# One partial sum of exponentials per half and head, a weight conversion that goes through PSUM banks, and nine buffers for exponentials

## The chip, the core and the metric

The kernel runs on one core of one Trainium2 chip. The metric is the time of one execution on the device in microseconds. TensorE (PE in the profile; PEld is its loading of weights), VectorE (DVE), ScalarE (ACT), GpSimd (POOL) and SyncE (SP, which issues most DMAs) each work through a list of instructions of their own, in order, and wait for each other with semaphores.

## What is computed

Attention in which a query sees only keys of its own hash bucket, over 4 batches of 8 heads with 768 positions of 64 numbers, and then a two-layer network with a rational activation:

```python
mask = q_bucket[:, :, :, None] == k_bucket[:, :, None, :]
scores = np.where(mask, scale * np.matmul(q, k.transpose(0, 1, 3, 2)), -1000000000.0)
scores = scores - np.max(scores, axis=-1, keepdims=True)
attn = np.exp(scores)
attn = attn / (np.sum(attn, axis=-1, keepdims=True) + 1e-09)
x = heads_side_by_side(np.matmul(attn, v))
...
h = x @ w_in
g = (a0 + a1*h + a2*h*h + a3*h*h*h) / (1 + abs(b0)*abs(h) + abs(b1)*h*h + 1e-6)
return g @ w_out
```

The weights `w_in` and `w_out` come in 64 bits per number. The kernel turns them into a 32-bit number and splits that into a high and a low part for TensorE; this is the work that the text calls the conversion.

## The kernel before

**Pairs, halves, steps.** The 32 heads are worked on as 16 pairs `p`. The scores of a pair are made transposed, with keys on partitions: 2 halves of 384 queries by 6 tiles of 128 keys give 12 steps `s` (steps 0 to 5 are half 0, steps 6 to 11 half 1). A step makes the scores of both heads (`pss`, two matmuls for each head, L356 to L381), ScalarE writes their exponentials into a buffer `E`, and GpSimd adds the exponentials up. After each six steps `values` (L383) multiplies the six buffers by V in 24 matmul passes (`psv`), and `values_out` (L392) has ScalarE read the result (`col`, then `xo`).

**Sums.** Six key tiles of a half are added in two groups of three (`PARTS = 2`): for each group and head one add `acc<-E,E` and one `acc<-acc,E`. So a pair has 4 tiles `acc`, each for both heads, out of a ring of `ACCS = 5`. `sums` (L402), two and a half steps into the next pair, multiplies every `acc` of the pair by a matrix of ones on TensorE (`psu`), the two groups accumulating in PSUM, and ScalarE copies the result out (`sr`). Step 11 of pair 14 and all of pair 15 have the second head's adds on VectorE (L380).

**Work two pairs ahead.** In the same steps TensorE and VectorE find the row maxima of pair p+2: `psm` (two matmuls into one of two double banks), then VectorE's `TENSOR_REDUCE m<-psm`. After step 5 the 12 maxima of pair p+1 are transposed (`pst`) and VectorE turns them into rows (`mt`). VectorE also makes the low parts `lo` of q and k.

**The conversion** (`weights`, L433) runs over 32 pieces, about two in each pair: even ones of `w_in`, odd ones of `w_out`. A piece needs two ScalarE activations (`ws<-wr`, `wr<-wr`), VectorE's `TENSOR_SCALAR wr<-wr` (the sign bits), `SCALAR_TENSOR_TENSOR ws<-ws,wr` (shift and or), an integer add `ws<-wr,ws` on 16-bit limbs (in the profile `CUSTOM_DVE_ANT_0`, in the order `ISA`), then ScalarE's cast to the high part and VectorE's subtraction for the low part (`wi_lo<-ws,wi_hi` or `wr<-ws,wr`). All operands are in SBUF.

**PSUM.** One pool, `ps_b`, has three banks with tag `s` that the scores `pss`, the transposes `pst` and the sums `psu` take in turn, and one bank for `psv`.

**The order** is written out: each piece of work is put at a place `12*p + step` by the tables `FIRST`, `MID` and `LAST`, and the program is issued sorted by that number (L475 to L543). So a wait in one engine's list holds up all that stands behind it there.

After the attention, from 393.6 us on, the two-layer network runs. Its code and order are not touched. The helper that records instructions makes every row of the profile carry line 95.

Of the kernel before, what the change touches and what calls it, by code (L numbers as in the profile page):

```python
# [7 lines left out]
F32 = mybir.dt.float32  # L8
F32R = mybir.dt.float32r
BF16 = mybir.dt.bfloat16  # L10
I32 = mybir.dt.int32
# [23 lines left out]
BIG = 2.0 ** 60  # L35
CLAMP = 2.0 ** 40
PINNED = ("tensor", "vector", "scalar", "gpsimd", "sync")
PARTS = 2
ACCS = 5

MID = dict(
    group=6, values=[0.66, 0.05], values_out=[0.69, 0.06],
    maxima=[6.54, 7.17, 8.32, 9.1, 10.1, 11.02, 12.25, 13.03, 14.15, 15.17, 16.01, 17.43], sums=14.65, sums_store=17.37,
    high=[-0.975, 1.19], low=[1.06, 2.8, 3.35], bits=2.81, penalties=4.02, high_move=1.9, maskrows=4.03, second_low=-2.2,
    second_high=2.69, load_v=10.99, shift_turn=5.67, shift_rows=8.82, load=4.04, recips=[20.0, 35.02, 35.3],
    weights=[[1.44, 5.1, 5.5, 5.65, 5.68, 11.02, 11.035], [8.05, 11.03, 11.04, 11.5, 12.38, 14.29, 17.645, 19.32, 21.22]],
    weights_last=[0.5, 0.8, 1.0, 1.2],
)

# [125 lines left out]
def attention(ctx, tc, nc, raw, ps_b, tail, tokens, early, operands_to_terms, ffn, load, QF, KF, v, w_in, w_out, wo_d, ident, cst, ones, prj,  # L175
# [9 lines left out]
    sm = ctx.enter_context(tc.tile_pool(name="sm", bufs=1))  # L185
    ps_a = ctx.enter_context(tc.tile_pool(name="ps_a", bufs=2, space=PSUM))

    E = [ep.tile([P, 2, HQ + 2], F32, name=f"E{i}") for i in range(7)]
    for e in E:
        nc.gpsimd.memset(e[:, :, HQ : HQ + 2], TINY)  # L190

# [228 lines left out]
    def recips(bb):  # L420
# [9 lines left out]
        nc.sync.dma_start(r_d[bb].rearrange("h (x c) -> (h x) c", c=n), s)  # L430
        yield

    def weights(i):  # L433

        if i % 2 == 0:
            f, cc = divmod(i // 2, 4)
            sl = slice(f * 512, f * 512 + 512)
            src, hi, lo = w_in[cc * P : cc * P + P, sl], wi_hi[:, cc, sl], wi_lo[:, cc, sl]  # L440
        else:
            src, hi, lo = w_out[i // 2 * P : i // 2 * P + P, :], None, None
        r = sm.tile([P, 2 * 512], F32, tag="wr", name=f"wr{i}", bufs=2)
        t = sm.tile([P, 512], F32, tag="ws", name=f"ws{i}", bufs=2)
        if src.dtype == F32:
            nc.sync.dma_start(t, src)
            yield
        else:
            nc.sync.dma_start(r.bitcast(I32), src.bitcast(I32))
            yield  # L450
            hw, lw = r[:, 1:1024:2], r[:, 0:1024:2]
            nc.scalar.activation(t, hw, AF.Copy, scale=2.0 ** -112)
            yield
            nc.scalar.activation(lw.bitcast(I32), lw.bitcast(U32), AF.Copy, scale=2.0 ** -29)
            nc.vector.tensor_scalar(out=hw.bitcast(I32), in0=hw.bitcast(I32), scalar1=-(1 << 31), scalar2=None,
                                    op0=ALU.bitwise_and)
            yield
            nc.vector.scalar_tensor_tensor(out=t.bitcast(I32), in0=t.bitcast(I32), scalar=3, in1=hw.bitcast(I32),
                                           op0=ALU.logical_shift_left, op1=ALU.bitwise_or)
            yield  # L460
            nc.vector.tensor_tensor(out=t.bitcast(I32), in0=t.bitcast(I32), in1=lw.bitcast(I32), op=ALU.add)
            yield
        if hi is None:
            hi, lo = r[:, 0:512].bitcast(F32R), r[:, 512:1024].bitcast(F32R)
        nc.scalar.copy(hi, t)
        yield
        nc.vector.tensor_tensor(out=lo, in0=t, in1=hi.bitcast(F32), op=ALU.subtract)
        yield
        if i % 2 == 1:
            move(nc, wo_d[i // 2], r.rearrange("p (t c) -> p t c", t=2))  # L470
            yield
# [51 lines left out]
    for i in range(2 * NFC):  # L523
        o = 12 * (i // 2)
        w = list(FIRST["weights"][i]) if i < 2 else list(MID["weights"][i % 2])
        if i == 2:
            w = list(FIRST["third_weights"])
        if i == 2 * NFC - 4:
            w[0] = LAST["weights14"]
        if i == 2 * NFC - 3:  # L530
            w[5] = LAST["hi14"]
        if i == 2 * NFC - 2:
            w[1:3] = LAST["weights15"]
        if i == 2 * NFC - 1:
            w = w[:-4] + [w[-5] + x for x in MID["weights_last"]]
        spread(0, [o + x for x in w], weights(i))

    for c in range(3):
# [309 lines left out]
```

## Time and profile before

| | us |
|---|---|
| median of 3 runs (923.38 to 923.84) | 923.7 |
| span of the profiled execution | 921.5 |
| attention, to the first matmul of the network | 393.6 |
| network | 527.9 |
| PE busy | 915.5 |
| DVE busy | 841.5 |
| ACT busy | 653.8 |
| POOL busy | 426.3 |

The page gives the busy time of each engine, then the span in 40 slices with the busy share of each in tenths, then the chain of work that ended last, then groups of equal instructions. In a group, `out<-in` are the program's tiles, `x` counts instructions, and behind the bar stand busy time in us, the mean of one in ns, and the idle time of the engine just before them with what ended it. The sums' matmuls count twice there (128 in the program, x256 in the profile). The profiled span and the time of the profiled execution differ: 923.7 is the median time on the device, the span runs from the first to the last instruction.

### The profile page before, as it was taken

What the parts mean: (1) busy time and instruction counts of PE and PEld (TensorE: products, weight loads), DVE (VectorE), ACT (ScalarE), POOL (GpSimd) and SP (SyncE); (2) the same over time, 40 slices, a digit from 0 to 9 for tenths busy, and PEclk for the clock granted to TensorE, in tenths of its full rate; (3) what the DMA queues carried; (4) which work ended last, traced back from release to release, by engine and by line L of the source; (5) the groups of instructions that cost most, each with busy time, mean ns of one, the idle gap of its engine ahead of it and who ended that gap; (6) DMA issues with size and microseconds to landing.
All of it is one profiled execution on the core that took longest, in us unless ns stands there. A gap on an engine that the chain in (4) does not pass through costs nothing.

```text
span 921.5 us, 13665 instructions
## 1 busy us (share of the span) xinstructions
PE 915.5 (99%) x4671; PEld 699.2 (76%) x4671; DVE 841.5 (91%) x1022; ACT 653.8 (71%) x1227; POOL 426.3 (46%) x363
## 2 busy tenths in 40 slices
PE   9999999999999999999999999999999999999998
PEld 5567767676767676678888888888888888888886
DVE  6799989999899899788998999999999989998997
ACT  7467777777777776976767677767676777667664
POOL 7577777677777777712222222222222222322221
PEclk9999999999999999999999999999999999999999
DMA  7877878787878778555403000400040013001001
GB/s 205 210 214 224 234 205 240 219 236 214 240 209 235 199 213 242 158 191 163 138 1 108 31 1 1 137 1 0 1 137 1 1 43 95 1 1 46 1 0 47
DMA packets 51242, 111.57 MB, mean 121 GB/s; under 512 B 9346, under 2 KB 20214, under 8 KB 51172
## 3 DMA queue, kind: packets, MB, share of 16 engines
q1 hardware_dynamic: 50740, 110.47, 40.7%
q8 instruction: 37, 0.61, 0.3%
q14 instruction: 33, 0.27, 0.1%
q10 hardware_dynamic: 432, 0.23, 0.1%
HBM read 56.82 MB, written 21.17 MB: 85 GB/s over the span
## 4 chain that ended last, share of the span: by engine, by line
PE 99%; DVE 1%; issue 0%; ACT 0%; DVEq 0%
PE psh L95 28%; PE pso L95 28%; PE pss L95 15%; PE psv L95 14%; PE psm L95 8%; PE psu L95 2%; PE psb L95 1%; PE psw L95 1%; PE pst L95 0%; PE pst_None L95 0%; PE psb_first L95 0%; DVE m L95 0%; DVE ws L95 0%; DVE k L95 0%; DVE mb L95 0%
## 5 line engine op out<-in xcount | busy, mean ns | idle before, releaser
L95 POOL TENSOR_TENSOR gl<-c,gh 128x512 fp32r<-128x512 f32 x95 | 135.8, 1429 | 384.9 <-ACT gh L95 374.8
L95 PE MATMUL pso<-wo,gh 128*128 128x512 f32 x768 | 235.9, 389 | 0.0
L95 DVE TENSOR_REDUCE m<-psm 128x1 f32<-128x768 f32 x192 | 181.3, 953 | 28.7 <-PE psm L95 20.1
L95 ACT ACTIVATE E<-pss 128x384 f32<-128x384 f32 x384 | 167.1, 492 | 41.5 <-PE pss L95 33.5
L95 POOL TENSOR_TENSOR acc<-E,E 128x384 f32<-128x384 f32 x124 | 147.2, 1206 | 92.1 <-ACT E L95 92.1
L95 PE MATMUL pss<-q,k 128*128 128x384 f32 (+2 forms) x768 | 171.0, 346 | 0.2
L95 PEld LDWEIGHTS pso<-wo,gh 128*128 128x128 f32 x768 | 144.1, 188 | 29.9
L95 ACT ACTIVATE h<-psh 128x512 f32<-128x512 f32 x96 | 57.4, 598 | 133.1 <-PE psh L95 133.0
L95 PEld LDWEIGHTS pss<-q,k 128*128 128x128 f32 (+2 forms) x768 | 134.5, 190 | 21.3 <-issue 8.0
L95 PE MATMUL psh<-xh,wi_hi 128*128 128x512 f32 x384 | 149.6, 390 | 0.0
L95 PE MATMUL psh<-xl,wi_hi 128*128 128x512 f32 x384 | 149.4, 389 | 0.0
L95 PE MATMUL psh<-xh,wi_lo 128*128 128x512 f32 x384 | 149.4, 389 | 0.0
L95 PE MATMUL pso<-wo,gl 128*128 128x512 f32 x384 | 148.9, 389 | 0.0
L95 DVE SCALAR_TENSOR_TENSOR c<-c,ab,r 128x512 f32<-128x512 f32 x96 | 138.7, 1444 | 0.0
L95 POOL TENSOR_TENSOR acc<-acc,E 128x384 f32<-128x384 f32 x123 | 132.0, 1093 | 3.8 <-ACT E L95 3.4
L95 PE MATMUL psv<-E,v 128*64 128x385 f32 x768 | 131.9, 492 | 0.0
L95 PE MATMUL psm<-k,q 76*128 76x384 f32 (+1 forms) x384 | 101.0, 345 | 0.5 <-ACT q L95 0.2
L95 PEld LDWEIGHTS psv<-E,v 128*64 128x64 f32 x768 | 52.0, 137 | 65.1 <-issue 62.4
L95 DVE SCALAR_TENSOR_TENSOR w<-h,absb,w 128x512 f32<-128x512 f32 x96 | 72.8, 758 | 15.5 <-ACT w L95 15.2
L95 PEld LDWEIGHTS psh<-xh,wi_hi 128*128 128x128 f32 x384 | 72.0, 188 | 16.1 <-issue 1.2
L95 PEld LDWEIGHTS psh<-xl,wi_hi 128*128 128x128 f32 x384 | 72.1, 188 | 15.0
L95 PEld LDWEIGHTS pso<-wo,gl 128*128 128x128 f32 x384 | 72.1, 188 | 15.0
(77 smaller groups left out, 1212.9 us busy)
## 6 DMA issues: line engine op xcount, KB each, us to landing
q<-q SPq DMA_DIRECT2D x45, 192.0 KB
k<-k SPq DMA_DIRECT2D x45, 192.0 KB
wr<-w_in SPq DMA_DIRECT2D x16, 512.0 KB
wr<-w_out SPq DMA_DIRECT2D x16, 512.0 KB
wo_d<-wr SPq DMA_DIRECT2D x16, 512.0 KB
wo<-wo_d SPq DMA_DIRECT2D x16, 512.0 KB
qkf<-qT SPq DMA_DIRECT2D x16, 384.0 KB
qkf<-kT SPq DMA_DIRECT2D x16, 384.0 KB
```

The source lines that it names most:

```text
L95: return self.tc.keep_in_program_order(issue(*args, **kwargs))
```

## The change

With `PARTS = 1` all six tiles of a half go into one `acc` for each head; the ring has 3 tiles. There are nine buffers `E`. For pieces 3 to 27 of the conversion the sign bits go to a bank `psx` with tag `s`, shift-and-or reads and writes that bank, and the limb add reads it; a new ScalarE copy puts the high part into another such bank, `psz`, and VectorE's subtraction reads that. One number of the table moves the limb add of odd pieces ahead of the next maximum; the last piece keeps its old place.

```diff
-PARTS = 2
-ACCS = 5
+PARTS = 1
+ACCS = 3
+BANKED = (3, 28)
...
-    weights=[[...], [8.05, 11.03, 11.04, 11.5, 12.38, 14.29, 17.645, 19.32, 21.22]],
+    weights=[[...], [8.05, 11.03, 11.04, 11.5, 11.6, 14.29, 17.645, 19.32, 21.22]],
...
-    E = [ep.tile([P, 2, HQ + 2], F32, name=f"E{i}") for i in range(7)]
+    E = [ep.tile([P, 2, HQ + 2], F32, name=f"E{i}") for i in range(9)]
...
+    def bank(name):
+        return ps_b.tile([P, 512], F32, tag="s", bufs=3, name=name)
...
-            nc.vector.tensor_scalar(out=hw.bitcast(I32), in0=hw.bitcast(I32), scalar1=-(1 << 31), scalar2=None,
-                                    op0=ALU.bitwise_and)
+            x = y = bank(f"psx{i}").bitcast(I32) if BANKED[0] <= i < BANKED[1] else hw.bitcast(I32)
+            if not BANKED[0] <= i < BANKED[1]:
+                y = t.bitcast(I32)
+            nc.vector.tensor_scalar(out=x, in0=hw.bitcast(I32), scalar1=-(1 << 31), scalar2=None, op0=ALU.bitwise_and)
             yield
-            nc.vector.scalar_tensor_tensor(out=t.bitcast(I32), in0=t.bitcast(I32), scalar=3, in1=hw.bitcast(I32),
-                                           op0=ALU.logical_shift_left, op1=ALU.bitwise_or)
+            nc.vector.scalar_tensor_tensor(out=y, in0=t.bitcast(I32), scalar=3, in1=x, op0=ALU.logical_shift_left,
+                                           op1=ALU.bitwise_or)
             yield
-            nc.vector.tensor_tensor(out=t.bitcast(I32), in0=t.bitcast(I32), in1=lw.bitcast(I32), op=ALU.add)
+            nc.vector.tensor_tensor(out=t.bitcast(I32), in0=y, in1=lw.bitcast(I32), op=ALU.add)
...
-        nc.vector.tensor_tensor(out=lo, in0=t, in1=hi.bitcast(F32), op=ALU.subtract)
+        z = hi.bitcast(F32)
+        if BANKED[0] <= i < BANKED[1]:
+            z = bank(f"psz{i}")
+            nc.scalar.copy(z, hi.bitcast(F32))
+        nc.vector.tensor_tensor(out=lo, in0=t, in1=z, op=ALU.subtract)
...
-            w = w[:-4] + [w[-5] + x for x in MID["weights_last"]]
+            w = w[:-5] + [12.38 + x for x in [0.0] + MID["weights_last"]]
```

In the rows below the numbers in `pss8_6_1` are pair, step and head, in `psx16` the piece; numbers after the last underscore only tell tiles apart. In brackets stand the semaphores that a row waits for: `DVE_49` is VectorE's, `Activation_49` ScalarE's, `Pool_49` GpSimd's, the ones with DMA are transfers.

**Place A**, TensorE in pair 8 behind the values of half 0 (the transpose of the maxima, then steps 6 and 7). Before:

```order
L95 MATMUL pst9_None_2715<-cst_75,m9_2451 12x128 [waits DVE_49]
L95 MATMUL pss8_6_0_2724<-q1_8_1990,k1_8_2045 128x384
L95 MATMUL pss8_6_0_2724<-q2_8_2234,k2_8_2235 128x384
L95 MATMUL pss8_6_1_2728<-q1_8_1990,k1_8_2045 128x384
L95 MATMUL pss8_6_1_2728<-q2_8_2234,k2_8_2235 128x384
L95 MATMUL psm10_0_2733<-k1_10_2595,q1_10_2541 128x384 [waits DMAHW4_49,DMAHW5_49,DMAHW3_49,PE_49]
L95 MATMUL psm10_0_2733<-k1_10_2595,q1_10_2541 128x384
L95 MATMUL pss8_7_0_2737<-q1_8_1990,k1_8_2045 128x384 [waits DVE_49]
L95 MATMUL pss8_7_0_2737<-q2_8_2234,k2_8_2235 128x384
L95 MATMUL pss8_7_1_2741<-q1_8_1990,k1_8_2045 128x384 [waits Activation_49]
```

Now:

```order
L96 MATMUL pst9_None_2744<-cst_75,m9_2476 12x128 [waits DVE_49]
L96 MATMUL pss8_6_0_2753<-q1_8_2008,k1_8_2066 128x384 [waits DVE_49]
L96 MATMUL pss8_6_0_2753<-q2_8_2257,k2_8_2258 128x384
L96 MATMUL pss8_6_1_2757<-q1_8_2008,k1_8_2066 128x384 [waits DVE_49]
L96 MATMUL pss8_6_1_2757<-q2_8_2257,k2_8_2258 128x384
L96 MATMUL psm10_0_2762<-k1_10_2624,q1_10_2567 128x384 [waits DMAHW4_49,DMAHW5_49,DMAHW3_49,PE_49]
L96 MATMUL psm10_0_2762<-k1_10_2624,q1_10_2567 128x384
L96 MATMUL pss8_7_0_2766<-q1_8_2008,k1_8_2066 128x384 [waits Activation_49]
L96 MATMUL pss8_7_0_2766<-q2_8_2257,k2_8_2258 128x384
L96 MATMUL pss8_7_1_2770<-q1_8_2008,k1_8_2066 128x384 [waits DVE_49]
```

The banks differ. Before, steps 6 take two free banks and head 0 of step 7 the bank of `pst9`, once `mt9` has read it. Now step 6 head 0 takes the bank of `psz15` (waits for the subtraction), head 1 the bank of `pst9` (waits for `mt9`), step 7 head 0 the bank of step 6 head 0 (waits for its exponential) and head 1 that of `psx16` (waits for the limb add). The same pattern stands in pairs 2 to 13.

**Place B**, TensorE at the start of pair 9, behind the values of half 1 of pair 8. Before:

```order
L95 MATMUL pss9_0_0_2848<-q1_9_2272,k1_9_2326 128x384 [waits DMAHW6_49]
L95 MATMUL pss9_0_0_2848<-q2_9_2503,k2_9_2504 128x384 [waits DMAHW1_49]
L95 MATMUL pss9_0_1_2852<-q1_9_2272,k1_9_2326 128x384
L95 MATMUL pss9_0_1_2852<-q2_9_2503,k2_9_2504 128x384 [waits DMAHW7_49,DMAHW0_49]
L95 MATMUL psm10_6_2856<-k1_10_2595,q1_10_2541 128x384 [waits DMAHW5_49,DVE_49]
L95 MATMUL psm10_6_2856<-k1_10_2595,q1_10_2541 128x384
L95 MATMUL pss9_1_0_2861<-q1_9_2272,k1_9_2326 128x384
L95 MATMUL pss9_1_0_2861<-q2_9_2503,k2_9_2504 128x384
L95 MATMUL pss9_1_1_2865<-q1_9_2272,k1_9_2326 128x384 [waits Activation_49]
```

Now:

```order
L96 MATMUL pss9_0_0_2882<-q1_9_2294,k1_9_2351 128x384 [waits DMAHW6_49]
L96 MATMUL pss9_0_0_2882<-q2_9_2530,k2_9_2531 128x384 [waits DMAHW1_49]
L96 MATMUL pss9_0_1_2886<-q1_9_2294,k1_9_2351 128x384 [waits DVE_49]
L96 MATMUL pss9_0_1_2886<-q2_9_2530,k2_9_2531 128x384 [waits DMAHW7_49,DMAHW0_49]
L96 MATMUL psm10_6_2890<-k1_10_2624,q1_10_2567 128x384 [waits DMAHW5_49,PE_49]
L96 MATMUL psm10_6_2890<-k1_10_2624,q1_10_2567 128x384
L96 MATMUL pss9_1_0_2894<-q1_9_2294,k1_9_2351 128x384 [waits Activation_49]
L96 MATMUL pss9_1_0_2894<-q2_9_2530,k2_9_2531 128x384
L96 MATMUL pss9_1_1_2898<-q1_9_2294,k1_9_2351 128x384 [waits Activation_49]
```

Step 0 head 1 now takes the bank of `psz16` (waits for the subtraction). Step 1 head 0, which had a free bank, now takes that of step 0 head 0 and waits for its exponential; `psx17` holds the third bank. So it stands at the start of pairs 3 to 13; at the start of pairs 2 and 14 a row of step 1 waits for the limb add instead.

**VectorE at place B**, from the subtraction of piece 16 on. Before:

```order
L95 TENSOR_TENSOR wi_lo_127<-ws16_2598,wi_hi_126 128x512
L95 TENSOR_SCALAR wr17_2765<-wr17_2765 128x512
L95 SCALAR_TENSOR_TENSOR ws17_2766<-ws17_2766,wr17_2765 128x512
L95 TENSOR_REDUCE m10_2732<-psm10_6_2856 128x1
L95 ISA ws17_2766<-wr17_2765,ws17_2766 128x1024
```

Now:

```order
L96 TENSOR_TENSOR wi_lo_127<-ws16_2627,psz16_2857 128x512
L96 TENSOR_SCALAR psx17_2861<-wr17_2794 128x512
L96 SCALAR_TENSOR_TENSOR psx17_2861<-ws17_2795,psx17_2861 128x512
L96 ISA ws17_2795<-wr17_2794,psx17_2861 128x1024
L96 TENSOR_REDUCE m10_2761<-psm10_6_2890 128x1
```

Each of the four conversion rows now has one operand in a bank, and the limb add has moved ahead of the maximum of step 6.

More of the change, by code (lines that the diff above doesn't have):

```diff
@@ L45 @@
     second_high=2.69, load_v=10.99, shift_turn=5.67, shift_rows=8.82, load=4.04, recips=[20.0, 35.02, 35.3],
-    weights=[[1.44, 5.1, 5.5, 5.65, 5.68, 11.02, 11.035], [8.05, 11.03, 11.04, 11.5, 12.38, 14.29, 17.645, 19.32, 21.22]],
+    weights=[[1.44, 5.1, 5.5, 5.65, 5.68, 11.02, 11.035], [8.05, 11.03, 11.04, 11.5, 11.6, 14.29, 17.645, 19.32, 21.22]],
     weights_last=[0.5, 0.8, 1.0, 1.2],
```

## The prediction

> **What bounds the kernel now.** I read the page first: the share of each engine, then the chain that ended last.
>
> ```profile
> PE 915.5 (99%) x4671; PEld 699.2 (76%) x4671; DVE 841.5 (91%) x1022; ACT 653.8 (71%) x1227; POOL 426.3 (46%) x363
> ...
> PE 99%; DVE 1%; issue 0%; ACT 0%; DVEq 0%
> PE psh L95 28%; PE pso L95 28%; PE pss L95 15%; PE psv L95 14%; PE psm L95 8%; PE psu L95 2%; PE psb L95 1%; PE psw L95 1%; PE pst L95 0%; PE pst_None L95 0%; PE psb_first L95 0%; DVE m L95 0%; DVE ws L95 0%; DVE k L95 0%; DVE mb L95 0%
> ```
>
> TensorE is never idle to speak of, and `psu`, which the change halves, stands on the chain with 2%. The windows view over twelve pairs of the attention shows who could take over (columns: length, then busy us and instructions of each engine, granted clock, DMA):
>
> ```profile
> core 0: us, PE busy (x) PEld busy (x) DVE busy (x) ACT busy (x) POOL busy (x), PEclk, DMA share, GB/s
> 75.60:357.20 281.60, 281.60 (x1741) 198.31 (x1740) 253.76 (x292) 206.46 (x450) 213.41 (x193) 1.00 0.79 223
> ```
>
> A pair takes 281.6 / 12 = 23.47 us of TensorE without a gap, 21.1 of VectorE, 17.2 of ScalarE, 17.8 of GpSimd. So a matmul that goes saves its whole time, and a wait that TensorE gets costs its whole time. That is the account to draw up. 0.2% of the median is 1.85 us, about what a measurement of this kernel can tell from no change.
>
> **Saved: half of the sums' matmuls.** The timeline of TensorE at one sum and the row behind it:
>
> ```profile
> 216.48 1.50 PE L95 MATMUL psu<-acc,ones 128*32 128x384 f32 x16
> 217.79 1.47 PE L95 MATMUL psb<-qkf,prj 128*32 128x384 f32 x16
> ```
>
> Sixteen passes hold TensorE for 217.79 - 216.48 = 1.31 us. With one `acc` instead of two it is eight, 0.65 less. There are 16 sums: 16 x 0.65 = **10.4 us saved**, since nothing on TensorE waits there.
>
> **What one wait costs.** Of the new waits in the order rows above, the trace of before has both kinds, a score matmul that waits for an exponential and one that waits for `mt`:
>
> ```profile
> 359.86 0.86 PE L95 MATMUL pss<-q,k 77*128 77x384 f32 x4
> 360.88 0.50 ACT L95 ACTIVATE E<-pss 128x384 f32<-128x384 f32 x1
> 360.91 1.14 PE L95 MATMUL pss<-q,k 77*128 77x384 f32 x4
> 361.43 0.30 PEld L95 LDWEIGHTS pss<-q,k 77*128 77x128 f32 x2 [0.32 <-ACT E L95]
> 66.44 0.27 DVE L95 TENSOR_SCALAR mt_None<-pst_None 12x128 fp32r<-12x128 f32 x1
> 66.76 0.65 PEld L95 LDWEIGHTS pss<-q,k 77*128 77x128 f32 x4 [0.45 <-DVE mt_None L95]
> ```
>
> The exponential ends at 361.38, TensorE goes on at 361.43; `mt` ends at 66.71, TensorE goes on at 66.76: 0.05 from end to start. Four score matmuls with such a wait take 1.14 where an undisturbed four take 0.86. Of these 0.28 the wait itself is 0.18 (from the 361.25 at which the third of four, 0.175 apart, was due), and 0.10 is lost in restarting, since no weights were loaded ahead.
>
> **Place A, waits for `mt`.** The rows of pair 8, where the banks change hands:
>
> ```profile
> 226.61 0.28 PE L95 MATMUL pst_None<-cst,m 128*12 128x128 f32 x1
> 226.64 0.96 PE L95 MATMUL pss<-q,k 77*128 77x384 f32 x4
> 226.92 0.28 DVE L95 TENSOR_SCALAR mt_None<-pst_None 12x128 fp32r<-12x128 f32 x1 [0.28 <-PE pst_None L95]
> 227.08 0.34 PE L95 MATMUL pss<-q,k 77*128 77x384 f32 x1
> 227.13 0.67 DVE L95 CUSTOM_DVE_ANT_0 ws<-wr,ws 128x1024 uint16<-128x1024 uint16 x1
> 227.42 0.48 ACT L95 ACTIVATE E<-pss 128x384 f32<-128x384 f32 x1
> ```
>
> Head 1 of step 6 starts at 227.08 and will need `mt`, which ends at 227.20: it goes on at 227.25, 0.18 late, and with the restart 0.28. What is queued behind it, a maximum and step 7, moves by as much. Step 7 head 0, due 0.7 after 227.08, needs the exponential that ends at 227.90 and comes at 228.06: no wait. Head 1, 0.35 behind it at 228.41, needs the limb add, done at 227.80. The subtraction that head 0 of step 6 needs stands ahead of `mt` on VectorE, which was idle for 0.28 before `mt`: done. Twelve pairs: 12 x 0.28 = **3.4 us lost**.
>
> **Place B, waits for an exponential.** The start of pair 9:
>
> ```profile
> 237.15 0.97 PE L95 MATMUL pss<-q,k 77*128 77x384 f32 x4
> 237.29 0.16 ACT L95 COPY col<-psv 128x1 f32<-128x1 f32 x1 [1.06 <-PE psv L95]
> 237.97 0.48 ACT L95 ACTIVATE E<-pss 128x384 f32<-128x384 f32 x1
> 238.32 0.34 PE L95 MATMUL pss<-q,k 77*128 77x384 f32 x1
> ```
>
> ScalarE reads the values first, so the first exponential ends only at 238.45. Step 1 head 0, due at 238.32, now waits for it: 238.50, again 0.18 and 0.10 of restart. The next three rows are then clear of theirs. Eleven pairs: **3.1 us lost**. At the two starts (pairs 2 and 14) that wait for the limb add I put 0.15 each, between 0 and 0.7: **0.3**.
>
> **VectorE and GpSimd.** The conversion rows over these pairs, then one of them with minimum, median and maximum, and last the rows of the network in which an operand is in PSUM:
>
> ```profile
> L95 ACT CAST wr<-ws 128x512 fp32r<-128x512 f32 x12 | 7.7, 638 | 0.0
> L95 DVE SCALAR_TENSOR_TENSOR ws<-ws,wr 128x512 int32<-128x512 int32 x24 | 24.8, 1034 | 0.4
> L95 DVE CUSTOM_DVE_ANT_0 ws<-wr,ws 128x1024 uint16<-128x1024 uint16 x25 | 17.0, 681 | 0.0
> L95 DVE TENSOR_TENSOR wr<-ws,wr 128x512 fp32r<-128x512 f32 x12 | 17.0, 1416 | 0.0
> L95 DVE TENSOR_TENSOR wi_lo<-ws,wi_hi 128x512 fp32r<-128x512 f32 x12 | 14.4, 1196 | 0.0
> ...
> L95 DVE SCALAR_TENSOR_TENSOR ws<-ws,wr x32: 676/1232/1469, 44.8 to 393.8; 128x512 int32<-128x512 int32 x32
> ...
> L95 DVE TENSOR_TENSOR c<-psh,c x96: 676/684/692, 398.6 to 906.2; 128x512 f32<-128x512 f32 x96
> L95 DVE SCALAR_TENSOR_TENSOR c<-c,ab,psh x96: 746/748/749, 399.3 to 906.9; 128x512 f32<-128x512 f32 x96
> ```
>
> The added copy `psz` on ScalarE I price as the cast, 0.64; it lies under the values, where the `col` row above shows ScalarE idle for 1.06. Were that cover gone, every exponential behind it would come later and place B's wait grow by as much.
>
> With all operands in SBUF the same instruction takes 0.68 or 1.47; with one in PSUM 96 of 96 stay within 16 ns. So a piece gets cheaper by about 0.3 (1.03 to 0.75) in shift-and-or and 0.5 to 0.7 in the subtraction; the sign bits I leave at their price. That is some 1.7 us a pair off VectorE's 21.1, all of it beside TensorE: worth nothing in itself, but needed for GpSimd. There four adds a pair come on top:
>
> ```profile
> L95 POOL TENSOR_TENSOR acc<-E,E 128x384 f32<-128x384 f32 x97 | 115.1, 1207 | 70.9 <-ACT E L95 70.9
> L95 POOL TENSOR_TENSOR acc<-acc,E 128x384 f32<-128x384 f32 x96 | 102.6, 1089 | 0.0
> ...
> 228.96 1.98 POOL L95 TENSOR_TENSOR acc<-E,E 128x384 f32<-128x384 f32 x2 [3.46 <-ACT E L95]
> 234.66 2.46 POOL L95 TENSOR_TENSOR acc<-acc,E 128x384 f32<-128x384 f32 x2
> 240.54 1.50 PE L95 MATMUL psu<-acc,ones 128*32 128x384 f32 x16
> ```
>
> At today's mix 20 adds need 17.8 x 20 / 16 = 22.2 us of a new pair of 23.47 - 0.65 + 0.56 = 23.4; undisturbed, at 0.97 (1.98 for two), 19.4. The half's last add ends at 237.12, 3.4 before the sum; two more adds leave 1.5. Nine buffers `E` let GpSimd be that late: at seven, one buffer was free beyond a half. Nothing waits, so no cost. Only pair 14, which has no maxima and is shorter, is tight:
>
> ```profile
> 375.13 1.00 POOL L95 TENSOR_TENSOR acc<-acc,E 128x384 f32<-128x384 f32 x1
> 375.20 1.35 DVE L95 TENSOR_TENSOR acc<-acc,E 128x384 f32<-128x384 f32 x1 [1.87 <-POOL acc L95]
> 377.36 1.50 PE L95 MATMUL psu<-acc,ones 128*32 128x384 f32 x16
> ```
>
> Its last add ends at 376.55, 0.8 before the sum. Two adds of 0.97 make that 378.5: the sum waits about 1.1 and 0.1 of restart, **1.2 us lost** (0 to 2, by how the adds collide with VectorE). The network's rows do not change: 0.
>
> **The sum.** -10.4 + 3.4 + 3.1 + 0.3 + 1.2 = -2.4 us: a span of 919.1 for 921.5. The median stands 2.2 above the span; I keep that distance: **921.3 us**, 0.26% faster.
>
> **Rivals.** *The waits cost less*, 17%. If a restart is free, the 23 waits cost 0.18 each and the time is 919.0; if none shows, because `mt` or the exponentials come earlier, 923.7 - 10.4 = 913.3 at the most. For it: only 0.18 us separates each from no wait. Against it: the order names these waits, and what they wait for starts when the values end, as before.
>
> *VectorE comes late*, 13%: the limb add reads PSUM now, and no row shows that at 16 bits. From the rows, 1024 elements at the pace of 512 in 0.684 would be at most 1.37 instead of 0.68; then at place A it ends at 227.13 + 1.37 = 228.50 against 228.41, and 12 rows wait 0.14 and restart for 0.10: +2.9, or 924.2. The Trainium skill, "VectorE: DVE Perf Modes", section "The perf-mode tier table", speaks for this: two-tensor operations run twice as fast on 16-bit data in SBUF, but at single pace with any operand in PSUM. By that rule this case is the likelier one for the add itself; no run here shows the limb add so yet. I keep it at 13% since 1.37 counts the fixed part of an instruction twice, and with it left out the add just makes it.
>
> *GpSimd becomes the bound*, 10%, the case on the other side. If the adds stay disturbed, by `lo` and by the conversion, they decide from 23.4 / 20 = 1.17 us each on. At the 1.207 of the group `acc<-E,E` a pair takes 24.1, 0.67 more than now, and 14 pairs make 933.1. For it: that group stands above 1.17 today. Against it: the mean of all adds is 213.4 / 193 = 1.11, and the instructions that disturb them are those that leave SBUF.
>
> **Numbers.** The forecast's own range, with the restart and pair 14 between their ends, is 919.6 to 922.9, at 60%. About 0.43 of that lies under 921.85, with the cheap waits 0.60 faster by over 0.2%; the rest of it and a late VectorE make 0.30 within 0.2%; GpSimd 0.10. The range for 8 in 10 takes in the restart for less than its price, where 919.0 is its end, some waits that don't show, and the late VectorE: 917.9 to 924.2.
>
> **What would show it.** `psu` x128 with about 12 us busy. At place A weight loads of `pss` that wait for `mt`, at place B for `E`, some 0.3 each and 12 and 11 times; one wait of `psu` near 375 for an add. The conversion's rows on VectorE at 0.68 to 0.75, the adds near 1.0. It is wrong if `pss` has no such waits, if `psu` waits in every pair, or if the limb add takes over 1.2 and `pss` waits for `ws`.

## The result, and the profile after

| | before | after |
|---|---|---|
| median, us | 923.6 | 934.3 |
| executions, us | 923.4 to 923.8 | 933.4 to 941.9 |
| profiled execution, its span, us | 923.7, 921.5 | 934.7, 932.9 |
| attention, to the first matmul of the network | 393.60 | 405.75 |
| granted clock over the span | 0.999 | 0.994 |

The changed kernel is slower: ratio 1.0134, 95% interval 1.0098 to 1.0170. The forecast was 921.3. A ratio and its interval come from single executions, one of which took 941.9 here, so that a ratio need not be the quotient of the medians (1.0115). The page of the changed kernel, its first line and its chain:

```profile
PE 919.2 (99%) x4543; PEld 694.1 (74%) x4543; DVE 831.8 (89%) x1024; ACT 665.6 (71%) x1252; POOL 463.5 (50%) x427
...
PE 86%; DVE 7%; issue 3%; DMA 2%; SPq 1%; ACT 1%; POOL 0%; DVEq 0%; ACTq 0%
```

TensorE still shows 99%, but the chain that ended last now passes through VectorE for 7% of the span, where it was 1%. The share of TensorE's busy time says nothing of this; the chain does. The same twelve pairs as in the prediction's window (columns as there):

```profile
78.20:365.70 287.50, 284.50 (x1645) 192.90 (x1644) 241.65 (x292) 217.70 (x473) 235.87 (x239) 0.99 0.77 217
```

They take 287.5 for 281.6. VectorE's load has indeed fallen, from 253.8 to 241.7, and GpSimd's has grown from 213.4 to 235.9.

**Where the 11.4 us of span went.** Both kernels issue the same matmuls in the same order, but for the sums. So each matmul's start can be set beside the start of the same one before; where the difference steps, time was lost or won. The steps, added up by place:

| place | forecast, us | measured, us |
|---|---|---|
| 16 sums of half the length | -10.4 | -10.4 |
| 24 waits at places A and B | +6.7 | +7.9 |
| start of pair 2, wait for the limb add | +0.15 | +2.3 |
| half clock behind it | 0 | +3.1 |
| `psm` that waits for `mb`, five even pairs | 0 | +3.1 |
| `psm` that waits for `m`, five odd pairs, 0.1 each | 0 | +0.6 |
| `psm` that waits for `m` in pair 1 | 0 | +0.7 |
| sum of pair 14 | +1.2 | +1.1 |
| two late exponentials in pair 15 | 0 | +2.2 |
| half clock behind them | 0 | +1.7 |
| start-up, before the first sum | 0 | -0.8 |
| sum | -2.4 | +11.5 |

The rows for them. First pair 8, from the adds of its first key tiles to `mb`, and places A and B:

```profile
221.72 1.99 POOL L96 TENSOR_TENSOR acc<-E,E 128x384 f32<-128x384 f32 x2 [1.71 <-ACT E L96]
222.71 1.81 DVE L96 TENSOR_TENSOR lo<-qkf,q 128x768 fp32r<-128x768 f32 x1
222.80 0.85 PE L96 MATMUL psu<-acc,ones 128*32 128x384 f32 x8
...
226.18 1.00 DVE L96 TENSOR_SCALAR mb<-psb,cst 128x768 fp32r<-128x768 f32 x1
...
227.24 0.62 PE L96 MATMUL psm<-k,q 76*128 76x384 f32 x2 [0.34 <-DVE mb L96]
...
233.53 0.30 PEld L96 LDWEIGHTS pss<-q,k 77*128 77x128 f32 x2 [0.34 <-DVE mt_None L96]
...
245.07 0.68 PEld L96 LDWEIGHTS pss<-q,k 77*128 77x128 f32 x4 [0.34 <-ACT E L96]
```

The last two rows are places A and B, as foretold: a weight load that waits 0.34 for `mt` and for `E`. The sum is shorter by 0.65 (222.80 to 223.47, where `psb` starts). What no step of the prediction had is the row at 227.24: TensorE waits for `mb` (VectorE's comparison of `psb`), since `lo` of q took 1.81 us instead of 0.95. Before, the same place read:

```profile
215.45 3.18 POOL L95 TENSOR_TENSOR acc<-E,E 128x384 f32<-128x384 f32 x2 [3.06 <-ACT E L95]
...
216.80 0.95 DVE L95 TENSOR_TENSOR lo<-qkf,q 128x768 fp32r<-128x768 f32 x1
...
219.40 1.01 DVE L95 TENSOR_SCALAR mb<-psb,cst 128x768 fp32r<-128x768 f32 x1
...
221.08 0.51 PE L95 MATMUL psm<-k,q 76*128 76x384 f32 x2
```

There GpSimd's two adds were the ones held up (3.18 for two instead of 1.99) and `lo` was not; `mb` ended at 220.41, and the `psm` that needs it came at 221.08. Second, the start of pair 2, and the granted clock behind it (in the second fence the columns of the windows view, the clock third from the end):

```profile
74.73 0.97 PE L96 MATMUL pss<-q,k 77*128 77x384 f32 x4 [1.97 <-DVE ws L96]
```

```profile
74.00:75.00 1.00, 0.27 (x1) 0.27 (x2) 1.00 (x2) 0.00 (x0) 0.00 (x0) 1.00 0.82 302
75.00:76.00 1.00, 1.00 (x6) 1.00 (x6) 0.54 (x1) 0.56 (x2) 0.00 (x0) 0.79 0.72 257
76.00:79.00 3.00, 3.00 (x16) 2.12 (x18) 2.62 (x3) 2.53 (x5) 2.99 (x3) 0.50 0.37 84
79.00:82.00 3.00, 3.00 (x24) 0.62 (x16) 1.53 (x2) 0.48 (x1) 2.26 (x2) 0.50 0.96 237
82.00:83.00 1.00, 1.00 (x8) 0.81 (x5) 0.65 (x1) 0.01 (x1) 0.00 (x0) 0.80 0.90 195
```

Step 1 of pair 2 takes the bank of piece 3, whose limb add ends at 74.68. TensorE stands for 1.97 us, then works at half clock; the shares make (0.21 + 1.5 + 1.5 + 0.20) / 0.5 = 6.8 us of half clock. Third, the end of the attention:

```profile
384.87 1.35 DVE L96 TENSOR_TENSOR acc<-acc,E 128x384 f32<-128x384 f32 x1 [3.51 <-POOL acc L96]
385.18 1.93 PE L96 MATMUL psu<-acc,ones 128*32 128x384 f32 x8
...
394.83 0.69 DVE L96 TENSOR_TENSOR y<-xl,xh 128x512 f32<-128x512 f32 x1
...
395.55 0.62 ACT L96 CAST xh<-y 128x512 fp32r<-128x512 f32 x1 [2.08 <-DVE y L96]
...
397.27 0.62 PE L96 MATMUL pss<-q,k 77*128 77x384 f32 x2 [1.15 <-ACT E L96]
...
398.42 1.90 PE L96 MATMUL pss<-q,k 77*128 77x384 f32 x8 [0.52 <-ACT E L96]
```

`y` is the attention's output multiplied by the reciprocals of its sums, and `xh` and `xl` are its high and low part. VectorE waits 3.5 us for GpSimd's late adds of pair 14, then has its own share of them, so `y` comes late; ScalarE's cast `xh` waits 2.08 for `y`, and the exponentials stand behind that cast. TensorE waits twice, and the clock is at 0.50 again from 400 to 403.

The conversion itself went as foretold:

```profile
L96 DVE SCALAR_TENSOR_TENSOR psx<-ws,psx 128x512 int32<-128x512 int32 x25 | 17.3, 690 | 0.5
L96 DVE TENSOR_SCALAR psx<-wr 128x512 int32<-128x512 int32 x25 | 17.1, 684 | 0.0
L96 DVE CUSTOM_DVE_ANT_0 ws<-wr,psx 128x1024 uint16<-128x1024 uint16 x25 | 16.9, 677 | 1.8
...
L96 DVE TENSOR_TENSOR lo<-qkf,q 128x768 fp32r<-128x768 f32 x13 | 21.9, 1681 | 0.0
L96 DVE TENSOR_TENSOR lo<-qkf,k 128x768 fp32r<-128x768 f32 x13 | 16.2, 1248 | 0.0
```

The first three, each with an operand in a bank, take 0.68 to 0.69; the two `lo`, which stayed in SBUF, went from 0.95 and 1.01 to 1.68 and 1.25. Before:

```profile
L95 DVE TENSOR_TENSOR lo<-qkf,q 128x768 fp32r<-128x768 f32 x13 | 12.4, 953 | 0.0
L95 DVE TENSOR_TENSOR lo<-qkf,k 128x768 fp32r<-128x768 f32 x13 | 13.1, 1009 | 0.0
```

### The profile page after: what moved, and what is told of

Read it like the earlier page. It is cut to its first block, busy times and chain, and to the rows that moved or that the text cites. A ratio compares the mean times of both kernels' runs of the same rounds, so it can differ in the third digit from the quotient of the medians.

```text
span 932.9 us, 13680 instructions
## 1 busy us (share of the span) xinstructions
PE 919.2 (99%) x4543; PEld 694.1 (74%) x4543; DVE 831.8 (89%) x1024; ACT 665.6 (71%) x1252; POOL 463.5 (50%) x427
## 4 chain that ended last, share of the span: by engine, by line
PE 86%; DVE 7%; issue 3%; DMA 2%; SPq 1%; ACT 1%; POOL 0%; DVEq 0%; ACTq 0%
PE psh L96 28%; PE pso L96 28%; PE pss L96 12%; PE psv L96 9%; PE psm L96 6%; DVE m L96 2%; DVE lo L96 1%; SPq L96 1%; DMA wr<-w_in 1%; PE psu L96 1%; DVE psx L96 1%; DVE ws L96 1%; DVE mb L96 1%; DMA q<-q 1%; PE psb L96 1%
## 5 line engine op out<-in xcount | busy, mean ns | idle before, releaser
L96 POOL TENSOR_TENSOR acc<-acc,E 128x384 f32<-128x384 f32 x247 | 250.1, 1047 | 8.1 <-ACT E L96 7.4
L96 PE MATMUL pso<-wo,gh 128*128 128x512 f32 x768 | 235.9, 389 | 0.0
L96 DVE TENSOR_REDUCE m<-psm 128x1 f32<-128x768 f32 x192 | 180.3, 952 | 27.1 <-PE psm L96 19.6
L96 PE MATMUL pss<-q,k 128*128 128x384 f32 (+2 forms) x768 | 177.1, 351 | 5.1 <-ACT E L96 2.2
L96 PEld LDWEIGHTS pss<-q,k 128*128 128x128 f32 (+2 forms) x768 | 132.3, 190 | 36.7 <-ACT E L96 12.1
L96 POOL TENSOR_TENSOR acc<-E,E 128x384 f32<-128x384 f32 x62 | 64.6, 1061 | 63.2 <-ACT E L96 63.1
L96 PEld LDWEIGHTS psh<-xh,wi_lo 128*128 128x128 f32 x384 | 72.1, 188 | 15.0
```

The source lines that it names most:

```text
L96: return self.tc.keep_in_program_order(issue(*args, **kwargs))
```

## The experiments

Each run is given with the median beside that of the kernel before in the same series, and the ratio with its interval. The first theory: four separate losses (the banks at A and B, the bank of piece 3, the adds at `lo`, the adds of pair 14), each with a repair of its own. Rivals: the banks cause it all, or the adds do.

### The two halves of the change

`sums_only`, the sums and the rings without the banks:

```diff
-BANKED = (3, 28)
+BANKED = (99, 99)
-    weights=[... 11.5, 11.6, 14.29 ...]
+    weights=[... 11.5, 12.38, 14.29 ...]
```

> The changed kernel with one partial sum per half, three acc and nine E, but no piece of the conversion in a bank and the limb add at its old place. My theory takes the 10.6 us by which the change came out slower apart into four: (a) the 2.0 us stall at the start of pair 2 and the half clock behind it, about 5, from the bank of piece 3; (b) the last exponentials of the attention that come late, about 5, from GpSimd's four more adds in pair 14; (c) matmuls psm that wait for mb in six even pairs, about 0.6 each, 3.6 in all, because more adds on GpSimd hold up lo on VectorE; (d) the waits at places A and B, some 7, from the banks. Then this kernel has only b and c: 923.6 - 10.4 + 5 + 3.6 = 921.8 us, clock 1.00 in the slice near 75 us, the wait for mb and the late exponentials still there. Rival 1, the banks cause everything that was lost: 923.6 - 10.4 = 913.2. Rival 2, the adds also cause the stall at pair 2, by making VectorE late there: 921.8 + 5 = 926.8.

Measured: 946.9 for 923.3, ratio 1.0254 (1.0239 to 1.0269). None of the three had it. The half of the change that takes work away from TensorE is by itself the slower one, by 23.6 us. Its timeline in pair 8:

```profile
212.76 7.22 POOL L96 TENSOR_TENSOR acc<-acc,E 128x384 f32<-128x384 f32 x8
...
214.89 5.64 DVE L96 TENSOR_TENSOR wi_lo<-ws,wi_hi 128x512 fp32r<-128x512 f32 x1
...
224.01 1.01 PE L96 MATMUL psm<-k,q 76*128 76x384 f32 x2 [2.97 <-DVE m L96]
```

The subtraction `wi_lo`, 0.68 when nothing is in its way, takes 5.64 us. It begins inside a row of eight adds on GpSimd (212.76 to 219.98) and ends at 220.53, half a microsecond behind the last of them: it is *held*. All that stands behind it on VectorE is late, and TensorE waits 2.97 for a maximum, until 224.01. Such a long hold happens five times in this kernel, to `wi_lo` (4.31, 5.64, 4.36) and to the short `rz` of the reciprocals (4.20, 5.28). Mostly the two engines take turns instead, as in pair 9, where the same instruction ends at 245.18, in the middle of a row of six adds that now take 1.08 each:

```profile
242.80 6.50 POOL L96 TENSOR_TENSOR acc<-acc,E 128x384 f32<-128x384 f32 x6
...
244.20 0.98 DVE L96 TENSOR_TENSOR wi_lo<-ws,wi_hi 128x512 fp32r<-128x512 f32 x1
```

`banks_only`, the other half:

```diff
-PARTS = 1
-ACCS = 3
+PARTS = 2
+ACCS = 5
-    E = [... for i in range(9)]
+    E = [... for i in range(7)]
```

> The changed kernel with two partial sums per half, five acc and seven E as before, but the conversion in banks and the limb add moved ahead. My theory: places A and B cost about 7, the stall at pair 2 with its half clock 5, nothing waits for mb and the last exponentials are in time: 923.6 + 7 + 5 = 935.6 us, with the half clock near 76 us in the page. Rival 2, the adds make VectorE late at pair 2: no stall there, 930.6. A third view, VectorE's cheaper conversion is worth something by itself: below 930.

Measured: 932.0 for 923.3, ratio 1.0095 (1.0080 to 1.0110). The even pairs take 24.69 for 24.08 in the mean and the odd ones 23.45 for 22.87, 0.6 more each: places A and B. At pair 2 TensorE stands for 1.15 us, and the clock stays full; so the half clock that I had put into the 935.6 was not there. The rows in which the first theory was wrong are these:

```profile
221.25 1.83 DVE L96 TENSOR_TENSOR lo<-qkf,q 128x768 fp32r<-128x768 f32 x1
...
224.74 1.00 DVE L96 TENSOR_SCALAR mb<-psb,cst 128x768 fp32r<-128x768 f32 x1
...
225.94 0.52 PE L96 MATMUL psm<-k,q 76*128 76x384 f32 x2
```

`lo` of q is long here as well, with 16 adds a pair. It isn't the four new adds: since the limb add has left SBUF, GpSimd's first adds run undisturbed, and `lo` meets them. With `psz` alone (below), where the limb add stands at the same place but works in SBUF, `lo` of q takes 1.03 in the mean. Before, 220.41 + 0.05 to 221.08 left 0.62 in hand; here 225.74 + 0.05 to 225.94 leaves 0.15. Take away the 0.65 of the shorter sum, and `psm` is 0.50 late. So the wait for `mb` needs both halves of the change, and in even pairs it gives back what the sum has saved.

Alone the halves cost 23.6 and 8.7, together 10.6, which is 21.7 less than their sum: so much of what the sums bring about the banks make good.

### Are the adds the cause?

`sums_few_adds`, the first of these kernels with 4 adds a pair for 20:

```diff
-        if kt % n > 0:
+        if kt == 1:
...
-    ... scalar=S * TINY, in1=s, op0=ALU.max, op1=ALU.add)
+    ... scalar=1.0, in1=s, op0=ALU.max, op1=ALU.add)
```

> The kernel with the sums alone (one partial sum, nothing in a bank), but GpSimd adds only the first two of the six key tiles, 4 adds a pair for 20; the other four tiles are left out of the sums, and every sum gets 1 added so that no division overflows. All matmuls, rings and conversions are as in the run with the sums alone (946.9). My theory: VectorE's conversion, lo and rz in SBUF are held for the whole length of a row of adds on GpSimd, up to 5.6 us, and that alone made that run slow. Without the row of adds no VectorE instruction there is held (wi_lo 0.7, rz 0.2 to 0.4, sign bits 0.4), the clock stays full, and the whole saving of the halved sums is left: 923.5 - 10.4 = 913 us. Rival: the loss comes from VectorE's own load or from the rings, and 925 or more remain.

Measured: 914.9 for 923.8, ratio 0.9901 (0.9889 to 0.9914), clock 1.00, 32 us less than with the adds. Groups of this kernel, and then of the one with all adds:

```profile
L96 DVE TENSOR_TENSOR wi_lo<-ws,wi_hi 128x512 fp32r<-128x512 f32 x16 | 10.7, 674 | 3.6 <-ACT wi_hi L96 3.6
...
L96 DVE TENSOR_SCALAR rz<-rs 128x48 f32<-128x48 f32 x4 | 0.7, 178 | 0.0
```

```profile
L96 DVE TENSOR_TENSOR wi_lo<-ws,wi_hi 128x512 fp32r<-128x512 f32 x16 | 28.0, 1753 | 0.0
...
L96 DVE TENSOR_SCALAR rz<-rs 128x48 f32<-128x48 f32 x4 | 10.4, 2594 | 0.0
```

This kernel leaves four of six key tiles out of its sums, so it is a test and no repair. With everything else the same, from pair 2 on no row of the conversion, no `lo` and no `rz` is held any more (two rows `y` still are, 1.76 and 1.63), and most of the saving of the halved sums shows: 8.9 of 10.4. TensorE's waits in the run with all adds are for maxima (19.4 us in 28 weight loads of `psm`), hardly ever for an add. So the adds cost by holding up VectorE, and that is nearly all of the 23.6 and of what the sums should have saved. A good part of it comes by way of the clock: in its profiled execution the kernel with all adds spends 30.7 us at half clock, with TensorE busy for 27.1 of them, which is some 13.5 us lost; with few adds there is none.

`no_extra_adds` left one key tile out of the changed kernel's sums, 16 adds a pair:

```diff
-        if kt % n > 0:
+        if kt % n > 0 and kt != 3:
```

> The changed kernel, but the fourth of the six key tiles is left out of the sums, so that GpSimd (and VectorE in the last pair) makes 16 adds a pair as before; every sum gets 1 added so that no division overflows. Banks, rings and all matmuls are as in the changed kernel. My theory, after the run with the sums alone (946.9) and with the banks alone (932.0): what the halved sums saved was lost by the four added adds a pair, which hold up VectorE. Without them: 932.0 - 10.4 = 921.6 us, no psm that waits for mb, the last exponentials in time, clock 1.00 at the end. Rival: the loss comes from the ring of three acc, the nine E or the new order, not from the adds' time: 930 or more.

Measured: 927.4 for 923.4, ratio 1.0041 (1.0029 to 1.0053). The end is in time, the wait at pair 2 is 1.3, and the clock is full at both places: 7 us less than the changed kernel. But the five waits for `mb` are all there (0.50 to 0.53), as the reckoning above wants it. So of the changed kernel's 10.6 us the four adds a pair are 7, and 4 are left when they are free.

### Repairing one wait

```diff
 from_4:         -BANKED = (3, 28)             +BANKED = (4, 28)
 share6:         -share=11                     +share=6
 compare_first:  -low=[1.06, 2.8, 3.35]        +low=[1.06, 2.82, 3.35]
 lo_early:       -low=[1.06, 2.8, 3.35]        +low=[0.27, 2.8, 3.35]
```

> The changed kernel with piece 3 left out of the banks, so that the first banked piece is 4. My theory: at the start of pair 2 no matmul of step 1 waits for the limb add of piece 3, TensorE does not stand for 2 us, and the clock stays full near 76 us: about 5 less, 929.3 us. Rival: VectorE is late in this stretch whatever piece is banked, the next one waits in its place, and the time stays at 934, with the clock falling some us later.

Measured: 932.1 for 923.3, ratio 1.0102 (1.0085 to 1.0119). The rival had half of it. A maximum waits at the same place, since piece 3's limb add, now in SBUF, still stands ahead of it (`psm` at 76.56, 1.60 idle); the clock stays full this time.

> The changed kernel, but VectorE makes the second head's adds from step 6 of pair 14 on, not only from step 11. My theory: in pair 14 GpSimd is busy all the time and late, VectorE waits for it 3.5 us at its own first add, and so y and the exponentials behind y on ScalarE come late. With the adds shared the wait of psu14 (1.1), the two waits for exponentials (2.2) and the half clock behind them (1.7) go: 934.3 - 5.0 = 929.3 us. Rival: VectorE, now with more adds of 1.35, is itself late with y, and nothing changes at the end: 934.

Measured: 929.3 for 923.4, ratio 1.0064 (1.0050 to 1.0078): the forecast 929.3. The sum of pair 14 doesn't wait, of the two late exponentials 0.7 us is left, the clock is full there. The end of the attention was GpSimd's lateness, passed on by VectorE.

> The changed kernel with one number moved, so that in even pairs VectorE makes the compare mb ahead of the low part lo of k and not behind it. My theory: psm waits for mb in five or six pairs only because lo of q and of k, held up by GpSimd's adds, stand ahead of it; with the compare one row earlier it is done 0.9 us sooner and the wait of 0.5 with its restart goes: 6 x 0.6 = 3.6 less, 930.7 us. Rival: the matmul then waits for the next thing in the same bank pair, or the low part comes too late for its transfers, and the time stays at 934 or grows.

Measured: 936.4 for 923.3, ratio 1.0143 (1.0122 to 1.0163). My theory fell:

```profile
128.96 1.00 DVE L96 TENSOR_SCALAR mb<-psb,cst 128x768 fp32r<-128x768 f32 x1
...
129.88 1.79 DVE L96 TENSOR_TENSOR lo<-qkf,k 128x768 fp32r<-128x768 f32 x1
...
132.60 0.61 PE L96 MATMUL psm<-k,q 76*128 76x384 f32 x2 [1.01 <-DVE m L96]
```

`mb` is early, but `lo` of k, one row later, now falls into a row of adds itself (1.61 in the mean, for 1.25), and the next `psm` waits twice as long for the maximum behind it.

> The changed kernel with one number moved: VectorE makes lo of q one maximum earlier (place 0.27 for 1.06), before GpSimd begins the first two adds of a half. My theory: lo of q takes 1.7 instead of 0.95 because it reaches VectorE while GpSimd is in these two adds and has to let them end; that lateness reaches mb, and five psm wait 0.5 and restart. Earlier, lo of q takes 0.95, and the waits for mb go: 934.3 - 3 = 931.3 us. Rival: the maximum that now stands behind lo is late instead, or GpSimd's other adds meet lo of k: 934 or more.

Measured: 932.8 for 923.8, ratio 1.0118 (1.0083 to 1.0153). In the profiled execution `lo` of q takes 0.99 in the mean and no `psm` waits for `mb`: from pair 3 to pair 13 the start difference to the kernel before, taken behind each sum, stays between 3.7 and 4.0, where in the changed kernel it grew from 4.1 to 7.8. Early on the move costs something, since a maximum of pair 1, now behind `lo`, comes 1.8 late. And then this:

```profile
351.56 7.20 POOL L96 TENSOR_TENSOR acc<-acc,E 128x384 f32<-128x384 f32 x8
...
353.73 5.08 DVE L96 TENSOR_SCALAR rz<-rs 128x48 f32<-128x48 f32 x1
```

The row at 353.73 works on 48 numbers a partition and took 0.38 to 0.66 at these places in the changed kernel. Here it reaches VectorE inside a row of adds and is let go when the row ends; the two stalls of TensorE and the half clock that follow cost 7.4 us (the start difference goes from 4.0 to 10.7 across one sum, which saves 0.65).

### One bank alone, and seven buffers

`psz_only` keeps sign bits and shift-and-or in SBUF, `psx_only` the subtraction:

```diff
 psz_only: -            x = y = bank(f"psx{i}").bitcast(I32) if BANKED[0] <= i < BANKED[1] else hw.bitcast(I32)
 psz_only: -            if not BANKED[0] <= i < BANKED[1]:
 psz_only: -                y = t.bitcast(I32)
 psz_only: +            x = y = hw.bitcast(I32)
 psz_only: +            y = t.bitcast(I32)
 psx_only: -        if BANKED[0] <= i < BANKED[1]:
 psx_only: -            z = bank(f"psz{i}")
 psx_only: -            nc.scalar.copy(z, hi.bitcast(F32))
```

> The changed kernel with the high part in a bank (psz), but sign bits and shift-and-or in SBUF as before. By the order no row at place A or B then waits for mt or for an exponential that has just begun, and no limb add holds a bank at pair 2. My theory: places A and B (6.5), the wait at pair 2 (2.2) and its half clock (3.1) go; VectorE loses 0.34 on each shift-and-or again, so that the waits of psm behind it get longer by some us: between 934.3 - 11.8 = 922.5 and 928. Rival: the shift-and-or in PSUM is what keeps VectorE ahead, and without it the maxima come late as in the run with the sums alone: 935 to 946.

Measured: 934.9 for 923.4, ratio 1.0115 (1.0086 to 1.0144). At the rival's lower end. Places A and B don't wait, but now a `psm` waits 0.4 to 0.8 in each pair, for a maximum behind the limb add and behind sign bits that were held:

```profile
99.48 1.98 DVE L96 TENSOR_SCALAR wr<-wr 128x512 int32<-128x512 int32 x1
```

> The changed kernel with sign bits and shift-and-or in a bank (psx), but without psz: the subtraction reads the high part from SBUF as before. My theory: the subtraction beside GpSimd's adds goes back to 1.2 to 1.4 from 0.68, more than the shift-and-or had given, and places A and B still wait, now for limb adds: slower than the changed kernel, 937 to 945 us. Rival: the hand-over of psz's bank is what the waits come from, and without it the time falls under 930.

Measured: 959.2 for 923.4 as the median of all six executions, which run from 947.0 to 967.4; the ratio, 1.0296 (1.0264 to 1.0327), is that of the three lowest, up to 956.1. Slower, as expected, and by more: in the profiled execution, the one of 947.0, `wi_lo` takes 1.69 in the mean and is held for 4.5 us three times. Of the two banks `psz` is the one that is needed most.

```diff
 seven_e:  -    E = [... for i in range(9)]    +    E = [... for i in range(7)]
```

> The changed kernel with seven buffers E instead of nine. My theory, as the prediction had it: with five adds in a row for each head GpSimd frees a half's buffers later, at the end of the half only one buffer is left over, and ScalarE's exponentials, TensorE's scores behind them, wait for adds in most halves: 940 us or more. Rival: GpSimd is never more than one buffer behind, and the time stays at 934.

Measured: 931.7 for 923.8, ratio 1.0089 (1.0076 to 1.0101). My theory, and the prediction's word that nine buffers let GpSimd be late, fell: exponentials wait for adds twice in the profile's waits, 0.6 us together, as in the kernel before, and the time is no longer. The buffers are neither the loss nor the cure.

### Several repairs at once

`repaired` joins `lo_early`, `from_4` and `share6`. `tidy` does the same with `lo` of q left in place for pair 3, piece 3's limb add at 12.38, and the reciprocals at step 5.6 (`recips=[20.0, 29.6, 29.9]`). `psz_late` is `psz_only` with the limb add at 12.38, `share=6` and `recips=[20.0, 30.45, 30.6]`; `psz_late_lo` has `low=[0.27, 2.8, 3.35]` besides.

> The changed kernel with three repairs at once: lo of q one maximum earlier, the bank of piece 3 left out, VectorE's share of the adds from step 6 of pair 14 on. My theory: the repairs add up, 934.3 - 3 (mb) - 2.2 (pair 2) - 5 (end) = 924 us, with places A and B left, 6.5, which is what keeps it from being faster than before. Rival: one repair's gain goes into the next wait: 927 or more.

> One partial sum, three acc and nine E, only psz in a bank, the limb add at its old place behind the maximum, VectorE's share of the adds from step 6 of pair 14 on, and the reciprocals of a batch at a place (step 6) where GpSimd is idle, since with psz alone a short VectorE instruction of theirs was held 5 us by a row of adds. My theory: no waits at A and B, the maximum is not behind the limb add (no 0.7 in each pair), no stalls that let the clock fall: 923.5 - 10.4 + some 4 of leftover waits = 917 us, faster than both. Rival: the sign bits in SBUF are held by the adds as in the run with psz alone (1.98 instead of 0.4), the maxima come late and the time is 925 or more.

> The kernel before it, with lo of q one maximum earlier as well. My theory: in that kernel lo of q is not held (1.0 with psz alone), so this changes little, 916 to 919 us. Rival: earlier lo pushes the maximum of step 1 back at a place where VectorE is just behind the sign bits, and psm waits: 3 or more us slower than its neighbour.

> The changed kernel with repairs that each answer to one wait seen in the runs: lo of q earlier in pairs 2 and on but not in the first of them (where it made a maximum late by 1.9), piece 3 in SBUF with its limb add behind the maximum (the wait at pair 2), VectorE's share of the last adds from step 6 of pair 14, and the reciprocals of a batch at a place where GpSimd is idle and VectorE waits anyway. My theory: what is then left against the kernel before is places A and B: 923.5 - 10.4 + 6.5 + some 1 to 2 of small waits = 921.5 us, faster than both kernels. Rival: VectorE instructions in SBUF still meet rows of adds by chance, one hold of 5 us and the half clock behind it cost 5 to 8, and executions spread from 922 to 932.

Measured: 940.7 (ratio 1.0150, 1.0112 to 1.0189), 938.6 (1.0149, 1.0126 to 1.0171), 955.3 (1.0359, 1.0329 to 1.0388) and 938.8 (1.0139, 1.0095 to 1.0182). None beats the kernel before, and the repairs don't add up. In `psz_late_lo`, by far the slowest, TensorE stands for a maximum once in every pair from 3 to 13, some 1.3 and 2.3 us in turn, and 47.8 us run at half clock: the rival. In `tidy` the start difference behind the sum of pair 12 is +4.3 us, less than the +7.8 of the changed kernel; then one hold takes it back:

```profile
340.58 7.21 POOL L96 TENSOR_TENSOR acc<-acc,E 128x384 f32<-128x384 f32 x8
...
342.38 6.23 DVE L96 TENSOR_TENSOR lo<-qkf,k 128x768 fp32r<-128x768 f32 x1
...
350.40 0.28 PE L96 MATMUL pst_None<-cst,m 128*12 128x128 f32 x1 [2.76 <-DVE m L96]
...
352.36 1.01 PE L96 MATMUL pss<-q,k 77*128 77x384 f32 x2 [1.69 <-DVE wr L96]
```

The two stalls and the half clock behind them (0.50 from 352 to 360, 0.60 in the mean of the ten microseconds that follow) cost 12 us. A second hold, of `xl` (5.57 at 377.62), costs 4.5 more. The executions of `tidy` run from 930.5 to 944.0, those of `repaired` from 932.2 to 942.2. The granted clock goes with them, in `tidy` from 0.998 down to 0.986, so that time at half clock is a large part of the difference. That the clock falls because a VectorE row is held in one execution and not in the next is argued, since only the profiled executions show holds. In `psz_late` the reciprocals at step 6 put back the maxima by their own 2.2 us, and TensorE waited 1.9.

## Why the prediction was wrong

- **The saving**: right. Each of the 16 sums is 0.64 to 0.65 shorter.
- **Places A and B**: right in kind, place and number; 0.33 each instead of 0.28, since at A some, and at B a third, were longer than 0.18 (0.34 at B). The run with the banks alone has them at 0.30.
- **Pair 14's sum**: right, 1.1 for 1.2. But I followed GpSimd's lateness only to the sum. VectorE's add there waits for GpSimd's (3.5), `y` stands behind it, ScalarE's cast behind `y`, the exponentials behind the cast: +2.2, which a walk along the queues would have shown, and +1.7 of half clock behind them.
- **Start of pair 2**: the wait was named and put at 0.15, at most 0.7; it was 2.3. The trace of before shows that limb add ending at 75.13, when step 1 had begun at 73.38. Moved ahead of the maximum in front of it, it would by estimate have ended near 74.3, a wait of 0.9: the row was there and I did not use it. The rest of the 2.3 is VectorE's lateness.
- **VectorE's conversion, "worth nothing in itself"**: wrong. I had it as needed for GpSimd, at no price; without it the sums cost 21.7 us more. The rival *VectorE comes late* fell in its own form: the limb add takes 0.68 from PSUM. By the Trainium skill, "VectorE: DVE Perf Modes", section "The perf-mode tier table", it would have run at single pace; the measurement decides, and this row, a custom instruction in the profile, did not.
- **GpSimd's adds, "Nothing waits, so no cost"**: this is the step that failed. The adds themselves came out as forecast (1.05 in the mean), and I asked only whether GpSimd would be in time for the sum. I did not ask whom the adds hold up. I read long VectorE rows (1.20, 1.42) and long adds (1.21) as prices; they are two sides of one conflict, and when the conversion leaves SBUF, GpSimd's rows of adds go through undisturbed and the next VectorE row in SBUF, `lo`, pays. Without most of the adds the sums alone give 914.9; with them 946.9. In the changed kernel the term that I put at nothing is 7 us for the four added adds (934.3 with them, 927.4 without), and the 3.1 us of waits for `mb` come from adds that were there before. The rival *GpSimd becomes the bound* gave 933.1, near to what came, but not by its mechanism, which needed adds of 1.17.
- **"Nothing on TensorE waits there"** for the sums: wrong in even pairs. `mb` was only 0.62 ahead of its `psm`. Here a saving of 0.65 on TensorE was worth no more than the spare time of the next engine that it met.
- **The network**: right, 527.9 before and 527.2 after, less by the last sum.
- **The clock** was left out: 4.8 us of half clock, behind waits that were left out too.

The Trainium skill, "GPSIMD Engine Reference", section "1. Specifications", says that GpSimd shares its SBUF interfaces with VectorE, and that VectorE rows with two SBUF inputs or in a two-port mode contend. The traces agree with whom it names: `lo`, `wi_lo` and `xl` have two SBUF inputs. `wr` and `rz` have one and are held too; no row shows in which mode they run. The traces also agree with whom it doesn't name: the sign bits that go into `psx` ran 0.675 to 0.690 in all 25 rows.

## What to carry to other kernels

Where GpSimd and VectorE both work in SBUF, count a GpSimd instruction twice: for GpSimd, and for the VectorE row that it may hold, mostly to the end of one add and now and then to the end of the whole row of them. Before a matmul is traded for adds on GpSimd, look for long variants of VectorE's rows in the trace (here 0.68 against 1.2 to 1.5); they tell that the two are already in each other's way. When each repair moves the loss to the next wait, suspect what all the waits share: here no repair of a wait made the kernel faster than before, and taking adds away did.

## What the hardware showed that I had not expected

**A long hold lasts to the end of the row.** Holds of 5.64, 5.28, 5.08 and 6.23 us were measured, and each ended 0.05 to 0.82 behind the last of a row of adds without a gap, which is the VectorE row's own time or less. They are rare. In the run with the sums alone 113 VectorE rows in SBUF began inside such a row of adds with another add to follow; 104 were done before that next add was, and five were held to the end. What decides between turns and a long hold these runs don't show.

**Half clock after a short wait, by chance.** A wait of 1.97 to 1.99 us stands at the start of pair 2 in six of the runs. Half clock followed it in four, among them the run with VectorE's larger share, but not in that with the earlier `lo` and not in that with seven buffers. The windows behind the wait with the larger share, and then with the earlier `lo`:

```profile
76.00:78.00 2.00, 2.00 (x13) 1.56 (x16) 1.46 (x2) 2.00 (x5) 1.55 (x2) 0.75 0.19 50
78.00:80.00 2.00, 2.00 (x16) 0.64 (x16) 2.00 (x3) 1.24 (x3) 2.00 (x2) 0.50 0.69 178
```

```profile
78.00:80.00 2.00, 2.00 (x12) 1.85 (x11) 2.00 (x3) 1.50 (x4) 0.93 (x1) 1.00 0.84 288
80.00:82.00 2.00, 2.00 (x25) 0.68 (x24) 2.00 (x3) 1.75 (x5) 2.00 (x3) 1.00 0.50 106
```

In the changed kernel the half clock lasted 6.8 us, and 3.4 at its second place. The Trainium skill, "TensorE: Matmul & The Clock Gate", section "Part 1: The HAM clock gate", has a gate that halves the clock after an idle window, and windows of 3.41 us that run freely. The traces agree with the lengths, once one window and once two, and with chance, by where the wait falls. A whole idle window was not needed: 1.98 us did it, and 1.60 in the run with `psz` alone. At the end of the attention two waits of 1.15 and some 0.5, half a microsecond apart, were enough in seven of the eight runs that have them. So there the measurement decides. Here a wait of 2 us cost 2 or 5.
